# Centroids first, loads held, first routing ahead of the angles: the front of a fused attention and FFT-gate kernel

## The chip, the cores and the metric

The kernel runs on one core of one Trainium2 chip. The metric is device time in microseconds (us), as the median of repeated runs. A profiled execution gives a trace of every instruction with its start, its duration and what released it. The engines are TensorE (PE, its weight loads are PEld), VectorE (DVE), ScalarE (ACT), GpSimd (POOL) and SyncE (SP). Names that end in q (SPq, ACTq) are the instructions with which an engine issues transfers.

## The reference

Two operators follow one another. The first is attention in which each query sees only keys of its own cluster; B, H, S, D = 4, 8, 768, 64 and there are 16 centroids per head.

```python
q_assign = argmax(einsum('bhsd,hcd->bhsc', q_n, c_n))     # q_n, k_n, c_n: rows of length 1
k_assign = argmax(einsum('bhsd,hcd->bhsc', k_n, c_n))
mask = q_assign[:, :, :, None] == k_assign[:, :, None, :]
scores = where(mask, q @ k.T / sqrt(D), -1e9)
x = softmax(scores) @ v                                   # then heads side by side: [4, 768, 512]
```

The second takes x through a projection, a long convolution by FFT over the 768 positions, two gates and an output projection.

```python
x1, x2, x3 = split(x @ w_proj, 3)                          # 512 columns each
y = x1 * irfft(rfft(x2) * rfft(filter_fft)) * x3
out = y @ w_out
```

## The kernel before

The work is tiled by pairs of heads: 16 pairs, `p` from 0 to 15, each with six steps of 128 keys. A pair first goes through `routing(p)`, then six calls of `attend(p, sk)`, then `finish(p)`. After every fourth pair one batch is whole, and `hyena(b, ...)` does the convolution and gates of it. `inverse_tables` and `filter_tables` make the Fourier tables `inv` and `hm` once, near the start; both use the table `fw` that `angles` makes with sines on ScalarE.

`centroid()` loads the centroids (L427), divides each by its length in a chain of small VectorE operations with one square root on ScalarE, turns the result over on TensorE (L440) and copies it into `cbd` (L445).

`routing(p)` turns q and k over on TensorE (L600, twelve tiles, copied to `qkT` by ScalarE or VectorE), casts them to bfloat16 into `aug` on GpSimd (L309), multiplies with `cbd` (L617), copies the similarities to `sim`, turns them over (L625), and finds the nearest centroid of each row with five VectorE operations (L630 to L636), whose result is the one-hot tile `oh`. This is turned over again (L644), scaled into `ohT` (L649 or L651), and four transfers (L658) put its rows into `aug` beside the data. There they act as the cluster mask: the score product over `aug` (L320, called S here) carries a large negative term where the clusters differ.

`attend` is S into the PSUM tile `scores`, an exponential on ScalarE into `pb` (L681, three buffers), the product with v into `outs` (L691, called PV here), and an addition on VectorE that sums `pb` for the denominators (L701). The scores tile is single: the next S waits for the exponential of the last.

PSUM has eight banks. `scores` holds banks 0 to 2, `outs` 3 and 4, and three more are free for everything else. The pool `psF` gives such work a bank: 5, 6 and 7 at all times, and those of `scores` and `outs` as long as no S has been planned.

No loop order reaches the hardware as written. Each operation is recorded by `op(...)` with the engines that it may run on, a duration, a due time, and an earliest time `after`. `Plan.run` then takes operations one by one: on each engine the one with the smallest due time plus a charge (`WAIT`) for what it would make the engine wait, less a bonus (`SAME`) where TensorE stays in its mode. The order in which it takes them is the order of the engines' instruction queues, and on the chip each engine and each transfer queue works through its own in order. `behind` adds operations that must be taken earlier. `step(i)` is the planned time of attention step i, `ROUTE`, `LOAD`, `TABLES`, `FILTER`, `ANGLES` and `SPANS` shift the due times of the parts against it.

The loads of a pair are recorded by `load_pair`: q and k for two heads each (192 KB each) and v (384 KB), on SyncE's queue; of pair 0, k goes by ScalarE's queue, ahead of the centroids. The last lines of the kernel record the parts in this order: loads of pair 0, constants, centroid, loads of pair 1, angles, zeros, weights, and then the pairs, each with its routing.

Of the kernel before, what the change touches and what calls it, by code (L numbers as in the profile page):

```python
# [87 lines left out]
class BankPool:  # L88
# [45 lines left out]
class Plan:  # L134
# [36 lines left out]
    def run(self):  # L171
# [13 lines left out]
        while ready:  # L185
            best = {}
            for o in ready:
# [42 lines left out]
            if o.size:  # L230
                wire = max(wire, done) + o.size / 2.0e5
                done = wire
# [28 lines left out]
def kernel(  # L261
# [105 lines left out]
    psS, psO, psF, psD = (BankPool(banks, x) for x in ("S", "O", "F", "D"))  # L367
# [11 lines left out]
    def load(dst, src, size, due, w, e="SP", after=0.0):  # L379
        op(e, 0.65, lambda e: eng[e].dma_start(dst(), src), w=[w], due=due, size=size, kind="load", after=after)  # L380

    raws, vraws = {}, {}

    def load_pair(p):
        b, h = p // 4, 2 * (p % 4)
        for j, src in enumerate((q, k)):
            x = raws[p, j] = Val(raw)
            for hp in range(2):
                load(lambda x=x, hp=hp: x.t[:, :, hp], src[b, h + hp].rearrange("(p t) d -> p t d", t=NT),
                     196608, step(6 * p - LOAD) + j if p else -1000.0, (x, hp), "ACTQ" if p == 0 and j else "SP",  # L390
                     after=step(6 * p - LOAD) - 8.0 if p > 1 else 0.0)
        x = vraws[p] = Val(vraw)
        load(lambda x=x: x.t, v[b, h:h + 2].rearrange("h (p t) d -> p h (t d)", t=NT),
             393216, step(6 * p - 3), x, after=step(6 * p - 6) - 8.0 if p else 2.0)
# [27 lines left out]
    def centroid():  # L422
# [4 lines left out]
        op("ACTQ", 0.1, lambda e: nc.scalar.dma_start(c.t, centroids.rearrange("h c d -> (h c) d")), w=[c])  # L427
# [11 lines left out]
        cps = Val(psF)  # L439
# [91 lines left out]
    def filter_tables(due):  # L531
        lo, hi, ud = Val(k6), Val(k6), Val(k6)
        fv = moe_filter_fft.rearrange("(w p m e) d -> w e p m d", w=2, p=64, m=3, e=2)
        for e_ in range(2):
            for x, w in ((lo, 0), (hi, 1)):
                load(lambda x=x, e_=e_: x.t.rearrange("p (m d) -> p m d", m=3)[64 * e_:64 * e_ + 64], fv[w, e_], 393216, due - 8.0, (x, e_),
                     after=due - 20.0)
# [41 lines left out]
    def weights():  # L579
        op("POOL", 1.2, lambda e: nc.gpsimd.dma_start(wpj.t, moe_w_proj.rearrange("(t p) m -> p t m", p=128)),  # L580
           w=[wpj], due=step(20), size=3145728, lag=3.0, after=step(4))
        op("POOL", 0.8, lambda e: nc.gpsimd.dma_start(wout.t, moe_w_out.rearrange("(t p) m -> p t m", p=128)),
           w=[wout], due=step(24), size=1048576, lag=3.0, after=step(8))
# [4 lines left out]
    def routing(p):  # L588
        due = step(6 * p - ROUTE) if p else FIRST - 400.0
        g = p % 4  # L590
        aug = augs[p] = Val(augp)
        qkT = [Val(qkTp) for _ in range(2)]
        for j in range(2):
            for ch in range(2):
                ps = Val(psF)

                def f(e, j=j, ch=ch, ps=ps):
                    rv = raws[p, j].t.rearrange("p t h d -> p t (h d)")
                    for t in range(3):
                        nc.tensor.transpose(ps.t[:, ts(t, 128)], rv[:, 3 * ch + t], identp.t)  # L600
# [9 lines left out]
        ps = Val(psF)  # L610
# [10 lines left out]
        sT, mx, cand, m2, oh, ohT = Val(psF), Val(mxp), Val(candp), Val(m2p), Val(ohp), Val(ohTp)  # L621
# [16 lines left out]
        oT = Val(psF)  # L638
# [15 lines left out]
        for j in range(2):  # L654
            for hp in range(2):
                def f(e, j=j, hp=hp):
                    r0 = 32 * j + 16 * hp
                    eng[e].dma_start(aug.t[hp][j][64 - 16 * hp:80 - 16 * hp], ohT.t[r0:r0 + 16])  # L658
                op("ACTQ" if p == 0 and j else "SP", 0.6, f, r=[ohT], w=[(aug, ("m", hp, j))], due=due - 0.5 * (1 - hp),
                   kind="mask", size=24576)  # L660
# [214 lines left out]
    load_pair(0)  # L875
    constants()
    centroid()
    load_pair(1)
    angles()
    zeros()  # L880
    weights()
    for p in range(NP):
        if p + 2 < NP:
            load_pair(p + 2)
        routing(p)
        if p == 0:
            inverse_tables(step(TABLES))
            filter_tables(step(FILTER))
# [35 lines left out]
```

## Time and profile before

| what | value |
|---|---|
| median of three runs | 429.64 us (428.15 to 429.93) |
| the profiled execution: its own time | 428.38 us |
| its span in the trace | 426.6 us |
| TensorE busy (matmul) | 397.4 us, 93% of the span |
| VectorE busy | 349.1 us, 82% |
| ScalarE busy | 255.1 us, 60% |
| GpSimd busy | 116.8 us, 27% |
| transfers | 37.17 MB, 87 GB/s over the span |

The page of the profile gives busy time by engine and the busy share in 40 slices of 10.7 us. Matmuls are pipelined, so a busy TensorE is not one at its peak. The timeline lists instructions in order of time, those alike merged (x6), with the idle time of the engine before them and what ended it in square brackets. The windows give the busy time of each engine in stretches that one names, with the granted clock of TensorE (PEclk) and the mean busy share of the transfer engines. The chain of waits follows the work that ended last back to what released it.

### The profile page before, as it was taken

What the parts mean: (1) busy time and instruction counts of PE and PEld (TensorE: products, weight loads), DVE (VectorE), ACT (ScalarE), POOL (GpSimd) and SP (SyncE); (2) the same over time, 40 slices, a digit from 0 to 9 for tenths busy, and PEclk for the clock granted to TensorE, in tenths of its full rate; (3) what the DMA queues carried; (4) which work ended last, traced back from release to release, by engine and by line L of the source; (5) the groups of instructions that cost most, each with busy time, mean ns of one, the idle gap of its engine ahead of it and who ended that gap; (6) DMA issues with size and microseconds to landing.
All of it is one profiled execution on the core that took longest, in us unless ns stands there. A gap on an engine that the chain in (4) does not pass through costs nothing.

```text
span 426.6 us, 8705 instructions
## 1 busy us (share of the span) xinstructions
PE 397.4 (93%) x3485; PEld 212.7 (50%) x3485; DVE 349.1 (82%) x411; ACT 255.1 (60%) x318; POOL 116.8 (27%) x115
## 2 busy tenths in 40 slices
PE   2759999999999999999999999999999999799875
PEld 2425454454545556655445455545544555465542
DVE  2885997998989888989988798899998598557763
ACT  2387657677677757555665676666667744144342
POOL 5660403355156240512204160507211020001000
PEclk9898999999999999999999999999999999899999
DMA  9979804546254414111357311021201012100213
GB/s 185 187 177 210 193 21 112 132 105 158 50 141 87 99 42 120 42 37 39 91 178 185 76 31 43 11 77 49 75 3 40 5 38 98 40 12 2 98 51 148
DMA packets 68943, 37.17 MB, mean 87 GB/s; under 512 B 56940, under 2 KB 62632, under 8 KB 68904
## 3 DMA queue, kind: packets, MB, share of 16 engines
q1 hardware_dynamic: 66072, 34.06, 31.7%
q0 software_dynamic: 1056, 2.10, 2.7%
q10 hardware_dynamic: 1776, 0.48, 0.6%
q8 instruction: 27, 0.44, 0.5%
q14 instruction: 12, 0.10, 0.1%
HBM read 30.66 MB, written 6.48 MB: 87 GB/s over the span
## 4 chain that ended last, share of the span: by engine, by line
PE 86%; DVE 9%; ACT 2%; DMA 2%; issue 1%; ACTq 0%; DVEq 0%
PE outs L691 30%; PE scores L320 21%; PE bank L320 18%; PE bank L600 5%; PE bank L720 3%; PE bank L617 2%; PE outs L320 2%; DVE tm L796 2%; PE bank L625 2%; DMA c<-in_centroids_dram 1%; PE bank L528 1%; PE bank L644 1%; DVE yy L852 1%; DVE k L485 1%; DVE m L635 0%
## 5 line engine op out<-in xcount | busy, mean ns | idle before, releaser
L681 ACT ACTIVATE pb<-scores 128x1536 f32<-128x1536 f32 x96 | 139.3, 1451 | 48.3 <-PE scores L320 46.6
L691 PE MATMUL outs<-pb,vraw 128*64 128x512 f32 (+1 forms) x768 | 143.2, 493 | 0.2 <-ACT osb L711 0.2
L701 DVE TENSOR_TENSOR acc<-acc,pb 128x1536 f32<-128x1536 f32 x64 | 121.3, 1895 | 15.3 <-ACT pb L681 14.3
L309 POOL CAST aug<-qkT 64x768 bf16<-64x768 f32 x64 | 77.7, 1215 | 127.0 <-PE scores L320 76.1
L691 PEld LDWEIGHTS outs<-pb,vraw 128*64 128x64 f32 x768 | 53.5, 137 | 69.9 <-issue 63.8
L320 PE MATMUL scores<-aug,aug 128*64 128x512 bf16 (+3 forms) x768 | 81.5, 330 | 0.3 <-ACT pb L681 0.3
L320 PEld LDWEIGHTS <-aug 80*64 80x64 bf16 (+1 forms) x768 | 42.5, 110 | 30.1 <-issue 13.9
L309 POOL CAST xT<-rb 128x768 bf16<-128x768 f32 x10 | 18.8, 1882 | 80.9 <-DVE rb L756 56.1
L320 PEld LDWEIGHTS <-wpj 128*64 128x64 bf16 x512 | 31.3, 110 | 19.0 <-issue 7.1
L701 DVE TENSOR_TENSOR acc<-pb,pb 128x1536 f32<-128x1536 f32 x16 | 29.4, 1835 | 9.2 <-ACT pb L681 9.2
L320 PE MATMUL bank<-xT,wpj 128*64 128x384 bf16 x360 | 36.3, 327 | 0.0
L600 PE MATMUL bank<-ident,raw 128*128 128x128 f32 x171 | 27.9, 292 | 6.4 <-DMA raw<-in_q_dram 6.4
L320 PEld LDWEIGHTS <-k 128*64 128x64 bf16 (+1 forms) x448 | 22.0, 110 | 23.8 <-issue 11.9
L855 POOL TENSOR_TENSOR k<-yy,x 128x768 bf16<-128x768 f32 x6 | 11.1, 1857 | 63.1 <-DVE yy L852 60.7
L600 PEld LDWEIGHTS bank<-ident,raw 128*128 128x128 f32 x171 | 19.1, 145 | 18.3 <-issue 8.2
L307 ACT COPY qkT<-bank 128x384 f32<-128x384 f32 x47 | 21.2, 480 | 8.6 <-PE bank L600 6.7
L320 PE MATMUL bank<-wpj,uT 128*64 128x512 bf16 x168 | 21.4, 380 | 0.0
L796 DVE TENSOR_TENSOR tm<-bank,hm 128x1024 f32<-128x1024 f32 x16 | 19.2, 1217 | 0.9 <-issue 0.8
L711 ACT COPY osb<-outs 128x769 f32<-128x769 f32 x16 | 12.8, 798 | 11.7 <-PE outs L691 11.7
L761 DVE TENSOR_TENSOR uT<-rb 128x384 bf16<-128x384 f32 x32 | 19.5, 622 | 0.0
L756 DVE SCALAR_TENSOR_TENSOR rb<-osb,rb 128x768 f32<-128x768 f32 x16 | 16.0, 1003 | 0.8 <-DMA rb<-dr 0.8
L307 ACT CAST k<-bank 128x512 bf16<-128x512 f32 x20 | 11.7, 585 | 8.3 <-PE bank L320 8.0
(167 smaller groups left out, 448.9 us busy)
## 6 DMA issues: line engine op xcount, KB each, us to landing
raw<-in_q_dram SPq DMA_DIRECT2D x32, 192.0 KB, 4.5
vraw<-in_v_dram SPq DMA_DIRECT2D x16, 384.0 KB, 3.7
raw<-in_k_dram SPq DMA_DIRECT2D x30, 192.0 KB, 3.4
rb<-dr SPq DMA_DIRECT2D x30, 192.0 KB, 3.5
out_dram<-os SPq DMA_DIRECT2D x21, 256.0 KB, 2.1
k<-in_moe_filter_fft_dram SPq DMA_DIRECT2D x4, 384.0 KB
wpj<-in_moe_w_proj_dram POOLq DMA_DIRECT2D x1, 1536.0 KB, 13.8
aug<-ohT SPq DMA_DIRECT2D x62, 24.0 KB, 1.8
```

The source lines that it names most:

```text
L307: nc.scalar.copy(o, i)
L309: eng[e].tensor_copy(o, i)
L320: nc.tensor.matmul(out[64 * c:64 * c + 64], lhsT[:, 64 * c:64 * c + 64], rhs, **k)
L600: nc.tensor.transpose(ps.t[:, ts(t, 128)], rv[:, 3 * ch + t], identp.t)
L681: op("ACT", 1.48, lambda e: nc.scalar.activation(pb.t[:, :, :S], sps.t.rearrange("p (a b) -> p a b", a=2), Act.Exp, scale=0.125), r=[sps], ...
L691: nc.tensor.matmul(o.t[64 * hp:64 * hp + 64, lo:hi], vv.t[:, hp, ts(sk, D)], pb.t[:, hp, lo:hi], start=(sk == 0), stop=(sk == NT - 1))
L701: nc.vector.tensor_tensor(acc.t, a, pb.t[:, :, :S], op=Alu.add)
L711: op("ACT", 0.82, lambda e: nc.scalar.copy(osb.t, o.t[:, :S + 1]), r=[o], w=[osb], due=step(i) + 5.0)
L720: nc.tensor.matmul(dps.t[32 * z:32 * z + 32, :384], ones.t[:, :32], acc.t[:, hp, ts(ch, 384)], start=True, stop=True)
L756: op("DVE", 0.98, lambda e: V.scalar_tensor_tensor(rb.t, osb.t[:, :S], osb.t[:, S:S + 1], rb.t, op0=Alu.add, op1=Alu.mult), r=[osb, rb], w ...
L761: op("DVE", 0.55, lambda e, e_=e_, alu=alu: V.tensor_tensor(uT.t[:, e_], x3()[:, :, :64], x3()[:, :, 64:], op=alu), r=[rb], w=[(uT, e_)], ...
L796: op("DVE", 1.2, lambda e, i=i, cs=cs, ps=ps, tm=tms[cs]: V.tensor_tensor(tm.t, ps.t.unsqueeze(1).to_broadcast([128, 2, DM]), hm.t[:, i, c ...
```

## The change

Six things change, all in what is recorded for the planner.

- The centroids are recorded before the loads of pair 0 and are the first transfer on ScalarE's queue; k of pair 0 goes by SyncE's queue, behind q.
- `load` takes `behind`, and the loads of q, k and v, the filter's loads and the weights are recorded with `behind=masks0`, the four transfers of the first one-hot rows.
- `routing(0)` is recorded ahead of `angles()`.
- The first routing and the centroids take their banks from a new pool, `psE`, which may use those of `scores` and `outs` until the first S. The pool `psF` of all other work loses the banks of `scores` in that time, and keeps those of `outs`.
- Constants of the planner: `LOAD` from 18.19 to 24.14, `ANGLES` from 1.84 to 0.99, the start of the second span from 60.4 to 63.3, v of pair 0 due at 8.0 and not before 4.0.
- The planner's own durations: 0.4 for the issue of the centroids, 0.15 or 0.1 for a change of mode in place of 0.095, and transfers on ScalarE's queue no longer take the planner's wire.

```diff
-ROUTE, LOAD, TABLES, FILTER = 3.96, 18.19, 0.98, 1.79
-SPANS = ((42.9, 50.0), (60.4, 100.2), (88.8, 116.7), (95.5, 135.3))
+ROUTE, LOAD, TABLES, FILTER = 3.96, 24.14, 0.98, 1.79
+SPANS = ((42.9, 50.0), (63.3, 100.2), (88.8, 116.7), (95.5, 135.3))
-SAME, WAIT, ANGLES = 1.08, 82.17, 1.84
+SAME, WAIT, ANGLES = 1.08, 82.17, 0.99
...
-        quiet = not b.scores_begun or not b.scores_left
-        last = not b.outs_left
-        ok = [5, 6, 7] + ([0, 1, 2] if quiet else []) + ([3, 4] if not b.scores_begun or last else [])
+        ok = [5, 6, 7]
+        if not b.scores_begun:
+            ok += [3, 4] + ([0, 1, 2] if k == "E" else [])
+        if not b.scores_left:
+            ok += [0, 1, 2]
+        if not b.outs_left:
+            ok += [3, 4]
...
-                    start += 0.095
+                    start += 0.15 if o.mode == "A" else 0.1
...
-            if o.size:
+            if o.size and e != "ACTQ":
...
-    def load(dst, src, size, due, w, e="SP", after=0.0):
-        op(e, 0.65, lambda e: eng[e].dma_start(dst(), src), w=[w], due=due, size=size, kind="load", after=after)
+    def load(dst, src, size, due, w, e="SP", after=0.0, behind=()):
+        op(e, 0.65, lambda e: eng[e].dma_start(dst(), src), w=[w], due=due, size=size, kind="load", after=after,
+           behind=behind)
...
-                     196608, step(6 * p - LOAD) + j if p else -1000.0, (x, hp), "ACTQ" if p == 0 and j else "SP",
-                     after=step(6 * p - LOAD) - 8.0 if p > 1 else 0.0)
+                     196608, step(6 * p - LOAD) + j if p else -1000.0, (x, hp),
+                     after=step(6 * p - LOAD) - 8.0 if p > 1 else 0.0, behind=masks0)
...
-        op("ACTQ", 0.1, lambda e: nc.scalar.dma_start(c.t, centroids.rearrange("h c d -> (h c) d")), w=[c])
+        op("ACTQ", 0.4, lambda e: nc.scalar.dma_start(c.t, centroids.rearrange("h c d -> (h c) d")), w=[c])
...
+        psX = psF if p else psE
...
-                op("ACTQ" if p == 0 and j else "SP", 0.6, f, r=[ohT], w=[(aug, ("m", hp, j))], due=due - 0.5 * (1 - hp),
-                   kind="mask", size=24576)
+                x = op("ACTQ" if p == 0 and j else "SP", 0.6, f, r=[ohT], w=[(aug, ("m", hp, j))],
+                       due=due - 0.5 * (1 - hp), kind="mask", size=24576)
+                if p == 0:
+                    masks0.append(x)
...
-    load_pair(0)
     constants()
     centroid()
+    load_pair(0)
     load_pair(1)
+    routing(0)
     angles()
```

`masks0` is a list that `routing(0)` fills, and `behind` is read when an operation is recorded. The loads of pairs 0 and 1 are recorded ahead of `routing(0)` and so are not held; those of pairs 2 and later, the filter's and the weights are. In the built program q and k of pairs 0 and 1 and v of pair 0 stand on SyncE's queue ahead of its two mask transfers, and v of pair 1 and all other loads behind them.

More of the change, by code (lines that the diff above doesn't have):

```diff
@@ L366 @@
                   [psum.tile([128, 512], F32, name=f"bank{i}") for i in range(3)])
-    psS, psO, psF, psD = (BankPool(banks, x) for x in ("S", "O", "F", "D"))
+    psS, psO, psF, psD, psE = (BankPool(banks, x) for x in ("S", "O", "F", "D", "E"))
     banks.scores_left, banks.outs_left = NP * NT, NP
@@ L536, in filter_tables @@
                 load(lambda x=x, e_=e_: x.t.rearrange("p (m d) -> p m d", m=3)[64 * e_:64 * e_ + 64], fv[w, e_], 393216, due - 8.0, (x, e_),
-                     after=due - 20.0)
+                     after=due - 20.0, behind=masks0)
         fu = lambda: ud.t.bitcast(BF16)[:, :1536]
@@ L580, in weights @@
         op("POOL", 1.2, lambda e: nc.gpsimd.dma_start(wpj.t, moe_w_proj.rearrange("(t p) m -> p t m", p=128)),
-           w=[wpj], due=step(20), size=3145728, lag=3.0, after=step(4))
+           w=[wpj], due=step(20), size=3145728, lag=3.0, after=step(4), behind=masks0)
         op("POOL", 0.8, lambda e: nc.gpsimd.dma_start(wout.t, moe_w_out.rearrange("(t p) m -> p t m", p=128)),
-           w=[wout], due=step(24), size=1048576, lag=3.0, after=step(8))
+           w=[wout], due=step(24), size=1048576, lag=3.0, after=step(8), behind=masks0)
     augs = {}
@@ L620, in routing @@
         op(("ACT", "DVE"), (0.486, 0.55), lambda e: copy(e, sim.t, ps.t[:, :384]), r=[ps], w=[sim], due=due)
-        sT, mx, cand, m2, oh, ohT = Val(psF), Val(mxp), Val(candp), Val(m2p), Val(ohp), Val(ohTp)
+        sT, mx, cand, m2, oh, ohT = Val(psX), Val(mxp), Val(candp), Val(m2p), Val(ohp), Val(ohTp)
         def f(e):
@@ L637, in routing @@
            r=[cand, m2], w=[oh], due=due, shared=True)
-        oT = Val(psF)
+        oT = Val(psX)
         def f(e):
@@ L884 @@
             load_pair(p + 2)
-        routing(p)
-        if p == 0:
+        if p:
+            routing(p)
+        else:
             inverse_tables(step(TABLES))
```

10 lines of the change are left out of this document (5 added, 5 removed).

## The prediction

> **What bounds the kernel now.** I read the windows first, to find where TensorE is not full, then the chain of waits in the front, then the timeline of it.
>
> ```profile
> 0.00:10.00 10.00, 2.79 (x12) 2.42 (x12) 2.21 (x12) 2.61 (x5) 5.53 (x24) 1.00 0.98 174
> 10.00:20.00 10.00, 6.78 (x41) 3.94 (x42) 7.97 (x18) 2.68 (x6) 6.01 (x8) 0.83 1.16 223
> 20.00:30.00 10.00, 6.76 (x46) 3.52 (x43) 9.18 (x16) 7.78 (x14) 6.62 (x15) 1.00 0.63 147
> 30.00:40.00 10.00, 8.07 (x71) 5.33 (x68) 5.05 (x9) 8.00 (x9) 2.14 (x3) 0.83 1.02 212
> 40.00:50.00 10.00, 10.00 (x85) 4.72 (x84) 9.81 (x8) 6.07 (x8) 3.04 (x2) 1.00 0.98 200
> ```
>
> The first number after the width is TensorE's busy time. It lacks 15.6 us up to 40 and nothing after that; the waits of TensorE from 34 to 380 us, the largest of which follows, are a few tenths in the attention and the rest near 360.
>
> ```profile
> PE scores L320 <- DVE tm L796: 2.2, 2, 1.4
> ```
>
> So from about 33 us on the kernel is bound by TensorE, and a change to the front is worth what it takes off the time at which TensorE becomes full, less the work that is then still undone. The chain of waits and the timeline show what the front waits for.
>
> ```profile
> 0.75 2.75 SPq L380 DMA_DIRECT2D raw<-in_q_dram  x4
> ...
> 2.42 5.40 DMA c<-in_centroids_dram
> ...
> 6.36 2.16 PE L600 MATMUL bank<-ident,raw 128*128 128x128 f32 x9 [6.36 <-DMA raw<-in_q_dram]
> ...
> 11.05 0.33 DVE L438 TENSOR_SCALAR cn<-c,s 128x64 f32<-128x64 f32 x1
> ...
> 12.25 0.44 DVE L445 COPY cbd<-scores 64x64 f32<-64x64 f32 x2
> ...
> 12.83 1.50 PE L617 MATMUL scores<-qkT,cbd 128*32 128x384 f32 x8 [1.09 <-DVE cbd L445]
> 14.27 1.54 PE L600 MATMUL outs<-ident,raw 128*128 128x128 f32 x6
> ...
> 16.44 0.56 DVE L630 TENSOR_REDUCE mx<-bank 128x24 f32<-128x384 f32 x1 [1.57 <-PE bank L625]
> ...
> 18.61 0.56 DVE L636 TENSOR_TENSOR oh<-cand,m 128x384 bf16<-128x384 bf16 x1
> ...
> 20.26 0.99 ACT L649 ACTIVATE ohT<-scores,mk 64x768 bf16<-64x768 bf16 x1 [1.22 <-PE scores L625]
> ...
> 21.97 0.83 ACTq L658 DMA_DIRECT2D aug<-ohT  x1
> ...
> 26.93 0.88 PE L600 MATMUL scores<-ident,raw 128*128 128x128 f32 x6 [2.30 <-DVE cand L631]
> ...
> 29.43 0.84 PE L320 MATMUL scores<-aug,aug 80*64 80x512 bf16 x8
> ...
> 30.54 1.28 ACT L681 ACT_TABLE_LOAD   x1
> ...
> 31.84 1.45 ACT L681 ACTIVATE pb<-scores 128x1536 f32<-128x1536 f32 x1
> ...
> 34.99 1.45 ACT L681 ACTIVATE pb<-scores 128x1536 f32<-128x1536 f32 x1 [0.95 <-PE scores L320]
> 37.29 0.38 PE L320 MATMUL scores<-aug,aug 80*64 80x512 bf16 x1
> ```
>
> The centroids land at 7.82, and the first routing goes through the similarities at 12.83 to the one-hot tile, whose last mask transfer is issued at 21.97. S0, the first score product, could run soon after, but stands on TensorE's queue behind transposes of pair 3 (26.93) that wait for the `scores` banks, on VectorE work that itself stood behind the angles. It starts at 29.43; S2, the third, at 37.29.
>
> **The change part by part.** I follow the built program's queues with the durations above.
>
> *The centroids.* They are issued at 0.75 instead of 2.42, with nothing ahead of them on their queue. The present 5.40 us to landing is the upper bound; the lower is that of a mask transfer of nearly this size:
>
> ```profile
> DMA to landing us min/median/max: 2.2/2.2/2.2
> ```
>
> So they land between 2.95 and 6.15. I take 3.3, near the lower, since the load of q alone shares the wires. From landing to the end of `cn` VectorE's order is unchanged: 11.38 − 7.84 = 3.54, so `cn` ends at 6.85. The two copies into `cbd` now precede the 0.56 us copy of `qkT`, which they follow today: 12.69 − 11.38 − 0.56 = 0.75, to 7.6.
>
> *k of pair 0 goes behind q on SyncE's queue.* Two issues more there, some 0.7 us each: four loads took 2.75 us to issue. q then has the wires nearly alone, and with 0.4 MB at the 174 GB/s of the first window it lands no later than today's 6.36; k lands about 2 us behind the front of q. Its six transposes follow the centroids' one on TensorE: 6 × 2.16/9 = 1.44 from 7.15, to 8.6, and the last copy to 9.2. This is the new cover: centroids later than 3.3 cost the same amount, k later than 7.1 too.
>
> *First routing.* From the similarities (12.83) to the first maximum (16.44) stand the same operations, among them six transposes of pair 1: 3.61, from 9.25 to 12.85. VectorE has five angle operations ahead of that maximum, about 3.3 us from 9.2, so they fit, barely. Maximum to the end of `ohT` is 16.44 to 21.25, 4.81, so 17.65. The masks go out at once; the second on ScalarE's queue started 0.69 behind the first and lands 2.2 later: S0 at 20.6. Of the 8.8 us that it gains, 3.6 come from the routing and 5.2 from TensorE's order, for no work of pairs 2 and 3 stands before it now: their loads are issued only behind the masks on SyncE's queue.
>
> *ScalarE between the first two exponentials.* This is the wait that comes. The angles, still 5 to 6 us of VectorE behind the one-hot tile, end near 21.5, and the sines now stand between the first exponential and the second, with a table load on either side: four table loads in all, three today.
>
> ```profile
> L491 ACT ACTIVATE fw<-k,quarter 128x384 bf16<-128x384 f32 x3 | 1.8, 603 | 0.0
> L494 ACT ACTIVATE fw<-k 128x384 bf16<-128x384 f32 x3 | 1.5, 508 | 0.0
> L491 ACT ACT_TABLE_LOAD x1 | 1.3, 1283 | 0.0
> L681 ACT ACT_TABLE_LOAD x1 | 1.3, 1283 | 0.0
> ```
>
> The first exponential runs from 21.5 to 22.95; then 1.28 + 3 × 0.603 + 3 × 0.508 + 1.28 + 1.45 = 7.34, so the second ends at 30.3 and S2 starts there. Its lead over 37.29 is 6.9 to 7.0. Behind ScalarE wait S2 and the inverse tables; TensorE has in that gap S1, one one-hot transpose, twelve transposes of pair 2, one PV, a similarity and four groups of the inverse tables, some 6.6 us, if q and k of pair 2 have landed: issued from 19 us on, 1.2 MB with v of pair 1 at 200 GB/s is 6 us, to 27. That leaves it full from 25 on, nearly free of waits.
>
> *The work postponed.* Ahead of S2 today, and behind it in the changed program: pair 2's turned similarities (0.55), its one-hot transposes (0.52), two groups of inverse tables (2 × 0.53) and six transposes of pair 3 (0.88):
>
> ```profile
> 28.50 0.52 PE L644 MATMUL outs<-identb,oh 128*64 128x128 bf16 x6 [0.69 <-DVE oh L636]
> 28.95 0.55 PE L625 MATMUL outs<-ident,sim 128*128 128x128 f32 x3
> 33.15 0.53 PE L516 MATMUL bank<-identb,fw 128*64 128x128 bf16 x6 [0.40 <-DVE inv L309]
> ```
>
> Together 3.0 us, which TensorE does later, when it is full: 7.0 − 3.0 = 4.0 net.
>
> *The order of the rest.* The whole program is re-planned. Where only a PV stands between two score products, TensorE waits for the exponential:
>
> ```profile
> 56.47 0.84 PE L320 MATMUL scores<-aug,aug 80*64 80x512 bf16 x8 [0.25 <-ACT pb L681]
> ```
>
> There are two such short steps more, 0.5 us; changes of TensorE's mode are 187 for 184, under 0.3. I set 0.6, with ±1.5 for an end whose operations are the same and whose order differs. The new start of the second span and `LOAD` show only in this order.
>
> The sum: 7.0 − 3.0 − 0.6 = 3.4. The profiled execution took 428.38, so 425.0; the median shown is 1.26 above it, which would make 426.2. I forecast 425.6, between the two.
>
> **A cold TensorE.** At 14 to 16 and at 34 to 36 the granted clock is half:
>
> ```profile
> 14.00:16.00 2.00, 2.00 (x12) 1.73 (x9) 0.87 (x2) 0.63 (x2) 0.19 (x1) 0.50 1.13 228
> 34.00:36.00 2.00, 2.00 (x12) 1.12 (x10) 0.08 (x1) 1.05 (x2) 0.00 (x0) 0.50 1.07 201
> ...
> 34.70 2.42 PE L691 MATMUL outs<-pb,vraw 128*64 128x512 f32 x8
> ...
> 37.94 1.59 PE L691 MATMUL outs<-pb,vraw 128*64 128x512 f32 x8
> ```
>
> Those eight matmuls took 2.42 against 1.59, and with S1 ahead of them the stretch cost some 1.5 us, inside today's 37.29. In the changed front a slow stretch may fall behind S2 instead, and the gain is then 1.9. The Trainium skill, "TensorE: Matmul & The Clock Gate", Part 1, says that the clock is halved until about 3.4 us of sustained work, and again after a pause; by that rule the pause before S0 chills S0 and S1, which ScalarE's 7.34 us hide, and the sum stays. The trace agrees only in part: it grants full speed from 0 to 10 us.
>
> **The rivals.**
>
> *The filter's loads come late.* They move from 11.6 and 28.9 us to behind the loads of pairs 2 and 3, some 25 to 28, and meet the weights, which GpSimd issues near 30 as today.
>
> ```profile
> 28.94 1.20 SPq L380 DMA_DIRECT2D k<-in_moe_filter_fft_dram  x2
> ...
> 30.46 0.92 POOL L580 DMA_DIRECT2D wpj<-in_moe_w_proj_dram  x1
> ...
> 41.86 1.75 DVE L540 TENSOR_TENSOR k<-k,k 128x1536 bf16<-128x1536 f32 x1
> ...
> vraw<-in_v_dram SPq DMA_DIRECT2D x1, 384.0 KB, 14.3
> ```
>
> VectorE meets the filter's sum (L540) at about 38, ahead of the additions that free `pb`, with 1.3 us to spare until TensorE needs its result. Today's second pair landed without making it wait, 13 us after issue at most. By the 14.3 us of the v load beside them the last would land at 42.5: 3.3 us of stall, the gain gone, 428.3. By the 200 GB/s they land near 37. From 39.3 on each microsecond is lost.
>
> *The early S0 is empty.* On the other side: if the masks do not land early, S2 still stands 9.7 us behind S0, for the sines and two table loads now stand between. The gain of 7.0 less the 3.6 of later costs is gone when S0 is at 24.0. With centroids at their upper bound (2.85 later) it is 23.5; add VectorE, whose five angle operations then run under GpSimd's casts at 0.9 to 1.0 each, and 1.5 more is at hand: 25.0, or 429.4. With S0 at 26, which also takes masks stuck behind the loads, 430.4. For it speaks how tightly VectorE is packed; against it, that the mask transfers find no load in flight.
>
> *A switch of tables costs twice its load.* Each of the two between the exponentials at 2.56 instead of 1.28 puts S2 at 32.9, and the sum at 427.6. Against it: the exponential at 31.84 follows its 30.54 table load without a pause. The Trainium skill, "ScalarE: Activation LUTs", "What ACT_TABLE_LOAD costs", adds a drain of 1.38 us to the load of 1.283 and so speaks against the change, by 2.8 us here. The trace agrees with the load and shows no drain.
>
> **How the numbers follow.** A median of this kernel tells about 0.5% (2.1 us) from no change. The case above has 0.64, most of it faster, 422.5 to 427.5. Filter late: 0.13, about no change. Tables twice: 0.05, no change or just faster. Empty S0, or an order of the rest that loses more than 3 us: 0.18, 429 to 432. Faster 0.64, same 0.18, slower 0.18. For 8 in 10 the range must reach into the rivals: from 421.5, the lead undiminished by clock and order, to 430.5.
>
> **What would show it.** Right: centroids landing by 3.5, S0 near 20.6 with no transposes of pairs 2 and 3 ahead, exponentials 7.3 apart at 21.5 and 28.8, S2 near 30.3, TensorE full from there on and the filter's sum on VectorE without a wait. Wrong: S0 after 24, VectorE waiting for a transfer at the filter's sum, a slow clock beyond 30, or more than 4 us of TensorE's waits between 40 and 380.

## The result and the profile after

The changed kernel takes 423.38 us (median of four runs, 422.92 to 424.17) against 429.77 (428.15 to 429.93) before on the same chip: 0.9862 of the time, with a 95% interval from 0.9834 to 0.989. This ratio, like those below, is estimated from all runs and is not the quotient of the two medians. The forecast was 425.6, faster, within 421.5 to 430.5. The profiled execution took 422.92, with a span of 421.1. Lines of code behind the changed functions are shifted: S is now L324, the exponential L689, PV L699, the filter's sum L545, the spectrum multiplications L804.

The windows of the changed kernel, with the same columns as before:

```profile
0.00:10.00 10.00, 4.57 (x20) 2.99 (x21) 4.99 (x22) 2.92 (x5) 5.54 (x24) 1.00 0.85 177
10.00:20.00 10.00, 5.04 (x38) 2.55 (x33) 9.83 (x16) 4.32 (x8) 8.81 (x16) 0.91 0.09 28
20.00:30.00 10.00, 8.05 (x44) 4.82 (x45) 5.16 (x11) 8.70 (x11) 1.79 (x4) 0.57 1.04 214
30.00:40.00 10.00, 9.64 (x93) 5.00 (x91) 9.42 (x14) 6.43 (x9) 3.27 (x4) 1.00 1.05 216
```

TensorE lacks 12.7 us up to 40 where it lacked 15.6. The sixth group, the granted clock, is 0.57 from 20 to 30: this front runs its first score products at about half speed. In the second window the transfers have a share of 0.09, since the loads are held. The timeline shows the first routing:

```profile
2.57 0.23 DVE L433 TENSOR_TENSOR c<-c 128x64 f32<-128x64 f32 x1 [0.99 <-DMA c<-in_centroids_dram]
...
8.60 2.72 PE L623 MATMUL scores<-qkT,cbd 128*32 128x384 f32 x8
...
13.43 0.54 DVE L636 TENSOR_REDUCE mx<-scores 128x24 f32<-128x384 f32 x1
...
17.06 0.99 ACT L655 ACTIVATE ohT<-scores,mk 64x768 bf16<-64x768 bf16 x1 [1.65 <-PE scores L650]
...
20.34 1.49 PE L324 MATMUL scores<-aug,aug 80*64 80x512 bf16 x8 [2.85 <-DMA aug<-ohT]
...
21.87 1.45 ACT L689 ACTIVATE pb<-scores 128x1536 f32<-128x1536 f32 x1 [1.24 <-PE scores L324]
...
25.52 1.54 PE L606 MATMUL bank<-ident,raw 128*128 128x128 f32 x6
26.99 2.26 PE L699 MATMUL outs<-pb,vraw 128*64 128x512 f32 x8
27.52 1.28 ACT L689 ACT_TABLE_LOAD   x1
28.81 1.45 ACT L689 ACTIVATE pb<-scores 128x1536 f32<-128x1536 f32 x1
...
32.14 0.84 PE L324 MATMUL scores<-aug,aug 80*64 80x512 bf16 x8
...
39.88 1.75 DVE L545 TENSOR_TENSOR k<-k,k 128x1536 bf16<-128x1536 f32 x1
```

S0 is at 20.34, and the wait that ends last before it is that for the masks; the two exponentials are 6.94 apart; S2 is at 32.14 where it was at 37.29; the filter's sum has no wait in front of it. S2 follows tables, similarities and transposes on TensorE without a pause, 1.88 us behind the end of the second exponential (30.26). The waits of TensorE from 33 to 345 us (total, count, longest) are small:

```profile
PE bank L650 <- DVE oh L642: 1.3, 1, 1.3
PE scores L324 <- ACT pb L689: 0.7, 2, 0.4
PE outs L699 <- ACT osb L719: 0.2, 1, 0.2
```

The surprise is at the other end of the kernel. Here is the timeline of before (rows of TensorE and VectorE) from the last denominators, L741, to the first projection of the last batch, which makes `outs` from `wpj` and `uT`; after it the timeline of the changed kernel with the same stations:

```profile
349.50 1.46 PE L741 MATMUL scores<-acc,ones 128*64 128x384 f32 x8
...
363.93 0.84 PE L528 MATMUL scores<-k,fw 128*64 128x512 bf16 x6
365.34 0.84 PE L528 MATMUL scores<-k,fw 128*64 128x512 bf16 x6 [0.57 <-ACT x L822]
367.55 1.85 PE L320 MATMUL scores<-wout,k 128*64 128x512 bf16 x8 [1.37 <-DVE tm L796]
369.13 1.98 PE L320 MATMUL outs<-wout,k 128*64 128x512 bf16 x8
...
369.44 1.23 DVE L796 TENSOR_TENSOR tm<-scores,hm 128x1024 f32<-128x1024 f32 x1 [1.94 <-PE scores L320]
...
373.25 0.84 PE L320 MATMUL outs<-wpj,uT 128*64 128x512 bf16 x6
```

```profile
348.45 1.48 PE L749 MATMUL scores<-acc,ones 128*64 128x384 f32 x8
...
360.34 0.84 PE L533 MATMUL outs<-k,fw 128*64 128x512 bf16 x6
360.99 0.84 PE L533 MATMUL scores<-k,fw 128*64 128x512 bf16 x6
...
362.42 1.21 DVE L804 TENSOR_TENSOR tm<-scores,hm 128x1024 f32<-128x1024 f32 x1
...
366.97 0.84 PE L324 MATMUL outs<-wpj,uT 128*64 128x512 bf16 x6
```

Of S2's 5.15 us only 1.05 are left at the last denominators (their place varies by about 1 us between executions of one order: with the changed order up to there it is 349.43 in e4_end_old, below). From there to the first projection of the last batch it is 23.75 before and 18.52 after, 5.23 less; from that projection to the last product 48.2 and 49.11, 0.91 more. In these two executions most of the gain therefore comes from a stretch that no line of the diff names.

### The profile page after: what moved, and what is told of

It reads as the page before. It is cut to its first block, busy times and chain, and to the rows that moved or that the text cites. A ratio compares the mean times of both kernels' runs of the same rounds, so it can differ in the third digit from the quotient of the medians.

```text
span 421.1 us, 8711 instructions
## 1 busy us (share of the span) xinstructions
PE 393.9 (94%) x3485; PEld 213.6 (51%) x3485; DVE 354.4 (84%) x414; ACT 256.5 (61%) x317; POOL 120.9 (29%) x114
## 5 line engine op out<-in xcount | busy, mean ns | idle before, releaser
L689 ACT ACTIVATE pb<-scores 128x1536 f32<-128x1536 f32 x96 | 139.4, 1452 | 52.2 <-PE scores L324 50.9
L699 PE MATMUL outs<-pb,vraw 128*64 128x512 f32 (+1 forms) x768 | 143.2, 492 | 0.2 <-ACT osb L719 0.2
L313 POOL CAST aug<-qkT 64x768 bf16<-64x768 f32 x64 | 85.1, 1329 | 160.6 <-PE scores L324 80.3
L709 DVE TENSOR_TENSOR acc<-acc,pb 128x1536 f32<-128x1536 f32 x64 | 118.1, 1845 | 9.5 <-ACT pb L689 9.1
L699 PEld LDWEIGHTS outs<-pb,vraw 128*64 128x64 f32 x768 | 54.4, 137 | 66.2 <-issue 59.7
L324 PE MATMUL scores<-aug,aug 128*64 128x512 bf16 (+3 forms) x768 | 81.8, 332 | 5.1 <-DMA aug<-ohT 2.8
L324 PEld LDWEIGHTS <-aug 80*64 80x64 bf16 (+1 forms) x768 | 42.1, 111 | 35.0 <-issue 15.5
L324 PEld LDWEIGHTS <-wpj 128*64 128x64 bf16 x512 | 32.3, 110 | 16.6 <-issue 5.6
L324 PE MATMUL bank<-xT,wpj 128*64 128x384 bf16 x384 | 38.5, 326 | 0.0
L709 DVE TENSOR_TENSOR acc<-pb,pb 128x1536 f32<-128x1536 f32 x16 | 31.8, 1987 | 4.7 <-ACT pb L689 4.7
L606 PE MATMUL bank<-ident,raw 128*128 128x128 f32 x183 | 30.5, 294 | 5.5 <-DMA raw<-in_q_dram 5.4
L324 PEld LDWEIGHTS <-k 128*64 128x64 bf16 (+1 forms) x448 | 21.7, 108 | 22.3 <-issue 11.4
L863 POOL TENSOR_TENSOR k<-yy,x 128x768 bf16<-128x768 f32 x7 | 16.1, 2302 | 58.6 <-DVE yy L860 54.1
L606 PEld LDWEIGHTS bank<-ident,raw 128*128 128x128 f32 x183 | 20.6, 147 | 20.1 <-issue 11.5
L313 POOL CAST xT<-rb 128x768 bf16<-128x768 f32 x8 | 10.6, 1325 | 45.3 <-PE bank L324 20.1
L769 DVE TENSOR_TENSOR uT<-rb 128x384 bf16<-128x384 f32 x32 | 21.4, 680 | 0.1
L324 PE MATMUL bank<-wpj,uT 128*64 128x512 bf16 x160 | 20.6, 380 | 0.0
L804 DVE TENSOR_TENSOR tm<-bank,hm 128x1024 f32<-128x1024 f32 x16 | 19.4, 1219 | 0.8 <-PE bank L533 0.7
L764 DVE SCALAR_TENSOR_TENSOR rb<-osb,rb 128x768 f32<-128x768 f32 x16 | 17.8, 1114 | 0.0
L324 PEld LDWEIGHTS <-uT 128*64 128x64 bf16 x192 | 12.6, 109 | 8.6 <-issue 1.9
```

Of the source, the lines that this page charges most:

```text
L313: eng[e].tensor_copy(o, i)
L324: nc.tensor.matmul(out[64 * c:64 * c + 64], lhsT[:, 64 * c:64 * c + 64], rhs, **k)
L689: op("ACT", 1.48, lambda e: nc.scalar.activation(pb.t[:, :, :S], sps.t.rearrange("p (a b) -> p a b", a=2), Act.Exp, scale=0.125), r=[sps], ...
L699: nc.tensor.matmul(o.t[64 * hp:64 * hp + 64, lo:hi], vv.t[:, hp, ts(sk, D)], pb.t[:, hp, lo:hi], start=(sk == 0), stop=(sk == NT - 1))
L709: nc.vector.tensor_tensor(acc.t, a, pb.t[:, :, :S], op=Alu.add)
L764: op("DVE", 0.98, lambda e: V.scalar_tensor_tensor(rb.t, osb.t[:, :S], osb.t[:, S:S + 1], rb.t, op0=Alu.add, op1=Alu.mult), r=[osb, rb], w ...
```

## The experiments

The planner's choices were written out as two tables, old and new, of the same 1563 operations (operation, engine, buffers), and the loop of `Plan.run` was replaced by one that takes operations in the order of a table. Experiments are tables put together from the two, or one of them with a few rows moved. All but e5_warm, which adds products that nothing reads, do the same work. Their code lies lower in the file: L372 (L371) is L324 of the changed kernel, L581 is L533, L593 is L545, L662 (L653) is L606, L795 is L749, L850 (L849) is L804. "Before" is each time the median of before on the same chip. The experiments ran on several chips, so differences of under 1 us between runs of different groups are read with care.

**Which part of the program the gain comes from.** Four tables, cut either at the first S of pair 4 (some 100 us) or at the last denominators:

```diff
 e1_front_new:  -old            +new to pair 4's first S, old behind it
 e2_front_old:  -new            +old to pair 4's first S, new behind it
 e3_end_new:    -old            +old to the last denominators, new behind them
 e4_end_old:    -new            +new to the last denominators, old behind them
```

> The order of the changed program up to the start of pair 4's first score product, the order of the old one from there on. If the front carries the whole gain, as the prediction has it: about 424, 5 to 6 us under before. If the front carries only what its trace shows (S2 5.15 us earlier, 3.0 us of work postponed): about 427.5, 2 us under before, and the rest comes from the order of the end.

> The mirror: the old order up to pair 4, the changed program's order from there on. If the front carries the whole gain: no change, 429. If the end carries some 4 us: about 425.5, 4 us under before.

> The old order up to the last pair's denominator product, the changed program's order for what is left (some 75 us). By the two traces this stretch up to the last batch's first projection took 22.3 us before and 17.2 after, with one group of gate products (0.65) fewer: if that is a matter of its order, 4 us under before, 425.5; if it follows from what the middle left over, no change, 429.

> The changed program up to the last denominator product, the old order for what is left. If the order of the end carries 4 us: 427.5, 4 us above the changed kernel; if the front carries all: 423.5, as the changed kernel.

| table | front, to pair 4 | middle | end | us | ratio, 95% |
|---|---|---|---|---|---|
| before | old | old | old | 429.5 | 1 |
| e1_front_new | new | old | old | 427.6 | 0.9968 (0.9944 to 0.9993) |
| e4_end_old | new | new | old | 427.87 | 0.9961 (0.9944 to 0.9978) |
| e2_front_old | old | new | new | 426.0 | 0.9924 (0.9907 to 0.9941) |
| e3_end_new | old | old | new | 425.37 | 0.9911 (0.9889 to 0.9933) |
| after | new | new | new | 423.38 | 0.9862 (0.9834 to 0.989) |

The last row is the result above, whose own before was 429.77; the others ran together. Each of the four lies within 0.5 us of the time that its expectation gives for an end worth some 4 us.

The new end is worth 429.5 − 425.37 = 4.1 with all else old and 427.87 − 423.38 = 4.5 with all else new. All ahead of it is worth 1.6 (429.5 − 427.87) or 2.0 (425.37 − 423.38), and the middle nothing that shows (427.6 to 427.87, 425.37 to 426.0). The stretch from the last denominators to the first projection keeps to the end's order, whatever stands ahead of it; first e3_end_new, then e4_end_old:

```profile
351.90 1.48 PE L795 MATMUL scores<-acc,ones 128*64 128x384 f32 x8
...
370.42 0.84 PE L372 MATMUL outs<-wpj,uT 128*64 128x512 bf16 x6
```

```profile
349.43 1.48 PE L795 MATMUL scores<-acc,ones 128*64 128x384 f32 x8
...
372.95 0.84 PE L372 MATMUL outs<-wpj,uT 128*64 128x512 bf16 x6
```

18.52 and 23.52 (the expectation of e3_end_new counts from the end of the denominators, hence its smaller numbers). The front is thus shown to be the smaller part of the gain.

**What in the end it is: the banks.** The three banks of `scores` are one tile. In the rows of before, ScalarE's copy, the spectrum products, the multiplications and the output product all use `scores`, and each waits for the one planned ahead of it: the second spectrum product (bank 2) for the copy (bank 0, 0.57), the output product (bank 0) for the first multiplication (bank 1, 1.37), the second multiplication (bank 2) for the output product (bank 0, 1.94). None of the three waits for its own bank.

```diff
 e9_one_bank, in the old table
-second spectrum product of the last block  bank 2 (scores)
-second output product behind it            bank 3 (outs)
+second spectrum product of the last block  bank 3 (outs)
+second output product behind it            bank 2 (scores)
```

> The kernel before, with two bank numbers exchanged near its end: the last of the six spectrum products of the third batch goes to bank 3, in the tile outs, instead of bank 2, in scores, and the second output product behind it to bank 2 instead of bank 3. Every engine's order of instructions is the old one. Theory (the three banks of scores are one tile, and every access to it, on whichever engine, waits for the one planned before it): TensorE no longer waits for ScalarE's copy between the two spectrum products (0.57) and waits less ahead of the output products (1.37); VectorE's second multiplication starts near 366 instead of 369.44, the stretch of half clock at 369 to 371 goes, and the time from the last denominators to the first projection of the last batch falls from 23.75 to 20 to 21.5: 426 to 427.5 in all, 2.3 to 3.7 less than before on the same chip. Rival (the order of the work there, how many projections stand behind the spectrum products, decides): the time stays within 0.7 of before, and the 23.75 stays above 23.

```profile
364.66 0.84 PE L581 MATMUL scores<-k,fw 128*64 128x512 bf16 x6
365.31 0.84 PE L581 MATMUL outs<-k,fw 128*64 128x512 bf16 x6
367.33 1.92 PE L372 MATMUL scores<-wout,k 128*64 128x512 bf16 x16 [1.18 <-DVE tm L850]
```

428.29, 0.9978 (0.9962 to 0.9994): 1.2 less than 429.47. The wait of 0.57 and the half clock are gone (both output products take 1.92 together, where they took 1.85 and 1.98), the second multiplication follows the first at 367.19, 2.25 sooner although the denominators are 0.7 later, and the stretch falls from 23.75 to 22.47. Part of what is won goes to two other waits of `scores` products for ScalarE's copies of the outputs, 0.67 and 0.72 behind 369, where before has one of 0.27. That is between what the two sides expected: the shared tile costs, but one bank is not the whole of it.

**What in the end it is: the order.**

```diff
 e12_end_order, in the table of e4_end_old
 last denominators
+both spectrum products of the middle block
 output products, projections ...
-both spectrum products of the middle block
 ...
-projection A
 both spectrum products of the last block
+projection A
+projection B
 two output products
-projection B
```

> New order up to the last denominators and the old order behind them, with three things moved within that old end as the new one has them: the two spectrum products of the second frequency block of the third batch right behind the last denominators (their two multiplications and the addition on VectorE likewise earlier), and two projections of the third batch from ahead of the last block's spectrum products, and from behind the output products, to between the two. Bank numbers stay the old ones except for the four products that this needs. Theory (the end gained by the order: the convolution's multiplications start earlier, and two projections fill TensorE's wait for the last of them): from the last denominators to the first projection of the last batch 18.5 to 20.5 instead of 23.52, and 423.5 to 425.5 in all against the 427.87 of the same order without the moves. Rival (the bank numbers and the half clock that follow from them): 22.3 to 23.5, and 426.8 to 428.

425.93, 0.9929 (0.9916 to 0.9943), 1.9 less than e4_end_old; against the before of its own chip (428.75) it gains 2.8 where e4_end_old gained 1.6, so 1.2 is the safer figure. From its timeline, rows of TensorE and VectorE:

```profile
365.61 1.49 PE L581 MATMUL scores<-k,fw 128*64 128x512 bf16 x12
...
369.57 0.84 PE L372 MATMUL scores<-xT,wpj 128*64 128x384 bf16 x8 [1.83 <-DVE tm L850]
...
371.31 1.22 DVE L850 TENSOR_TENSOR tm<-scores,hm 128x1024 f32<-128x1024 f32 x1 [1.79 <-PE scores L372]
...
374.66 0.84 PE L372 MATMUL outs<-wpj,uT 128*64 128x512 bf16 x6
```

The last denominators are at 353.45 in this execution, so the stretch is 21.21: 2.3 of the 5.0 between 23.52 and 18.52 come with these moves, less than the theory wanted and more than the rival. The run moves the middle block's products and the two projections together and does not tell which counts. The last block's products now stand 12.2 us behind the denominators (14.4 in the old order, 11.9 in the new). With the old bank numbers the second multiplication still starts 5.7 us behind those products, 2.1 in the changed kernel. The other 2.7 lie in the bank numbers and the few rows not moved; how they divide was not run.

**A better version.** If the shared tile costs time in the last 40 us as well, new bank numbers alone should help the changed kernel.

```diff
 e11_banks, in the new table, 15 rows; among them, in the last batch
-spectrum products, middle block: 2, 0 (scores, scores)
-spectrum products, last block:   7, 2
-last output products:            0, 3 (scores, outs)
+spectrum products, middle block: 7, 5 (tiles of their own)
+spectrum products, last block:   7, 5
+last output products:            6, 7
```

> The changed kernel, with other bank numbers for 17 products of the last batch, chosen so that products whose readers are slow lie in tiles of their own (banks 5, 6, 7) and not beside others in scores or outs; every engine's order stays. Theory (false waits between the banks of one tile cost time in the end): TensorE's waits for tm at 385.6 (1.66) and 392.1 (1.31) shrink to under 0.7 each, the last multiplications end 2 to 4 us sooner, and the time is 419.5 to 422. Rival (VectorE's own work bounds that stretch, or the waits are real): 422.7 to 424.

The expectation speaks of 17 products; 15 rows of the table differ, 13 products of the last batch and two output products of the third.

419.43 (418.18 to 420.03), 0.9771 (0.974 to 0.9802): 4.0 less than the changed kernel, 3.7 when each is taken against its own before, with no instruction in another place. The multiplications of the last batch on VectorE, first the changed kernel, then this one:

```profile
390.84 1.22 DVE L804 TENSOR_TENSOR tm<-scores,hm 128x1024 f32<-128x1024 f32 x1 [1.55 <-PE scores L324]
393.00 1.23 DVE L804 TENSOR_TENSOR tm<-scores,hm 128x1024 f32<-128x1024 f32 x1 [0.93 <-PE scores L324]
...
400.12 1.23 DVE L807 TENSOR_TENSOR k<-tm,tm 128x1024 bf16<-128x1024 f32 x1
```

```profile
388.89 2.35 DVE L849 TENSOR_TENSOR tm<-bank,hm 128x1024 f32<-128x1024 f32 x2 [0.53 <-PE bank L371]
...
396.15 1.23 DVE L852 TENSOR_TENSOR k<-tm,tm 128x1024 bf16<-128x1024 f32 x1
```

Two waits for `scores` become one of 0.53, and the last addition is 4.0 earlier although the last denominators are 0.4 later (348.89). TensorE's waits for `tm` behind 380, 3.0 in the changed kernel, are 0.9.

**The front, part by part.** First the clock. Two windows of the changed kernel:

```profile
18.00:20.00 2.00, 0.00 (x0) 0.00 (x0) 1.97 (x5) 0.70 (x2) 1.37 (x2) 0.57 0.13 27
...
26.00:28.00 2.00, 2.00 (x9) 1.05 (x10) 1.33 (x3) 1.98 (x5) 0.28 (x1) 0.50 1.29 218
```

All windows of 2 us from 20 to 28 show 0.50. e5_warm adds products to keep TensorE busy around S0:

```diff
 one-hot transposes of pair 0
+16 products of 384 columns into a free bank
 S0
+8 products of 384 columns
 S1
```

> The changed kernel, order untouched, with 16 products of 384 columns that nothing reads on TensorE ahead of the first score product S0, and 8 more ahead of the second. They stand where TensorE is idle (17.5 to 20.3 and 21.8 to 23.4). If the half clock from 18 to 28.5 us is what puts S2 at 32.1 instead of 30.3, it is granted in full there now, S2 stands near 30.5 and the kernel gains up to 1.6 us over the changed one (422). If the pause is not what lowers the clock, or S2 is held by ScalarE's sines and table loads: no change or up to 0.5 us slower.

```profile
26.25 0.87 PE L662 MATMUL bank<-ident,raw 128*128 128x128 f32 x6 [2.12 <-DMA raw<-in_q_dram]
```

```profile
20.00:24.00 4.00, 3.54 (x31) 2.04 (x30) 3.22 (x7) 3.12 (x3) 0.00 (x0) 1.00 0.73 185
24.00:28.00 4.00, 1.88 (x15) 1.01 (x14) 1.69 (x3) 3.97 (x8) 0.01 (x1) 1.00 0.91 199
```

The clock stays at 1.00, S0 stays at 20.34, and S2 comes at 31.45, 0.7 sooner; 422.74, 0.9854 (0.9829 to 0.988), which can't be told from the changed kernel. At full clock TensorE has 2.1 us to spare from 24 to 28, waiting for q of pair 2 until 26.25, and behind that it has 5.2 us of transposes, PV, similarities and tables ahead of S2. In the changed kernel, at half clock, q is in use at 25.52 after a wait of 0.31. So the 0.7 is not the price of the half clock: with the clock up, the load of q takes its place as what holds S2. e8_unheld, below, is the other half of this.

Then the place of the first two score products. e6_sines_first puts the sines ahead of the first exponential (one table load less) and S1 and the first PV behind the transposes and tables:

```diff
-exp0, sines, exp1 on ScalarE; S0, S1, transposes, PV0, tables, S2 on TensorE
+sines, exp0, exp1 on ScalarE; S0, transposes, tables, S1, PV0, S2 on TensorE
```

> The changed kernel with the six sines on ScalarE ahead of the first exponential, so that one table load falls away, and with the second score product and the first PV behind the transposes of pair 2 and four groups of inverse tables on TensorE. If the wait of 7.3 us between the first two exponentials is the price of the new order: the second exponential ends about 1.3 us earlier (29.0), S2 follows, and the kernel gains about 1 us (422.5). If S2 is set by TensorE's slow clock and its own work before S2: no change. If the first score product was worth its early place: slower by 1 to 2 us.

425.99, 0.9914 (0.9885 to 0.9943), 2.6 more than the changed kernel, though the two intervals just touch: S1 moves to 31.30, the second exponential waits 5.50 us for it, and S2 moves to 33.68. The run moves the sines and, on TensorE, S1 and the first PV together, so it shows that the two early score products as a whole earn their place, and not what the sines alone cost.

Then the queues. In e7_k_first the two loads of k of pair 0 go back to ScalarE's queue. In the built program they stand there behind the centroids, not ahead of them, so it tests only which queue k takes, not the centroids' place; e10_k_ahead puts them ahead.

```diff
 e7_k_first:  ScalarE's queue  centroids +k +k     SyncE's queue  q q -k -k
 e10_k_ahead: ScalarE's queue  +k +k centroids     SyncE's queue  q q -k -k
```

> The changed kernel with k of pair 0 back on ScalarE's queue ahead of the centroids, all else as it is. The centroids then land some 5 us later (7.8 instead of 2.6) and the first routing and S0 follow by 3 to 4 us; as S2 stands 11.8 us behind S0, it comes at 35 to 36 and the whole gain of the front (1.5 to 2 us) is gone: 426 to 427. If S2 has slack, under 1 us lost.

> The changed kernel, with both loads of k of pair 0 on ScalarE's queue ahead of the centroids, as before the change; all else keeps its order. Theory (the transfers of one queue are done in order, so the centroids come 2 to 4 us later, and with them the whole first routing): centroids first used at 5 to 7 instead of 2.57, S0 at 22.5 to 24.5, S2 1.5 to 4 later than 32.14 and the time 425 to 427.5. Rival (the first routing is paced by k and by VectorE, and the centroids have slack): S0 within 1 us of 20.34 and the time within 1 us of the changed kernel's 423.4.

e7_k_first: 424.8, 0.9895 (0.9873 to 0.9918), 1.4 more than the changed kernel, at the edge of what the two intervals tell apart. The centroids are used at 2.64. With k on the other queue, and q of pair 1 next behind q of pair 0, q is there at 6.49 instead of 5.40; S0 follows at 21.48 and S2 at 33.65. e10_k_ahead: 428.32, 0.998 (0.9959 to 1.0), all but before's time:

```profile
7.23 0.23 DVE L481 TENSOR_TENSOR c<-c 128x64 f32<-128x64 f32 x1 [5.64 <-DMA c<-in_centroids_dram]
...
24.18 1.61 PE L372 MATMUL scores<-aug,aug 80*64 80x512 bf16 x8 [2.83 <-DMA aug<-ohT]
...
44.83 1.76 DVE L593 TENSOR_TENSOR k<-k,k 128x1536 bf16<-128x1536 f32 x1 [1.85 <-DMA k<-in_moe_filter_fft_dram]
```

The centroids come 4.66 later, S0 3.84, S2 (at 35.16) 3.0, the time 4.9. Part of that is the filter's load, which VectorE now meets 1.85 us before it has landed.

Last, the held loads:

```diff
 e8_unheld, SyncE's queue
+v of pair 1, q and k of pairs 2 and 3
 two mask transfers of pair 0
-v of pair 1, q and k of pairs 2 and 3
```

> The changed kernel with v of pair 1 and q and k of pairs 2 and 3 issued on SyncE's queue ahead of the first mask transfers instead of behind them. If holding them is what gets the masks through: masks and S0 1 to 3 us later. If the wires would be clear by 17 us in any case (2 MB from 8 us on at 200 GB/s ends at 18 to 19): S0 as it is, the transposes of pair 2 no longer wait for loads, 0 to 1 us gained.

424.46, 0.9902 (0.9872 to 0.9932). S0 is at 20.51 and S2 at 32.14 as in the changed kernel, though the transfers' share from 10 to 20 us is 1.14 instead of 0.09. Here the masks land as fast beside the loads; holding them buys S0 nothing. The transposes of pair 2 wait for no load now, but they start at 25.66 all the same, because the clock is 0.50 from 20 to 28 here too and the work ahead of them takes that long. The 1.1 by which the median is above the changed kernel's is not told from none: the two intervals overlap.

The two runs together say more than each alone. With the clock up and the loads as they are (e5_warm), q of pair 2 holds S2; with the loads early and the clock at half (e8_unheld), TensorE's slow work holds it. No run has both out of the way. An estimate from the rows of e5_warm: the one-hot transposes end at 24.13, 5.2 us of work behind them would end at 29.3, and the second exponential ends at 29.87, so S2 would start near 29.9 and wait for ScalarE, as I had forecast.

## Why the prediction was right, and where it was not

The sign, the range and, within 2.2 us, the time were right. The sum was not: the lead of the front was less than I had put, the end gained where I had put a loss, and the two went against each other. That the time came so near is luck to that extent: with the end's old order the same front takes 427.87, which is inside the range too, but only 1.6 under before.

- *The centroids and the first routing.* First use 2.57 for a landing at 3.3, `cn` at 6.15 for 6.85, similarities 8.60 for 9.25, `ohT` to 18.05 for 17.65, S0 20.34 for 20.6. The routing gave back more than the 0.65 of the similarities: its first maximum came at 13.43 for 12.85, behind similarities that took 2.72 where they had taken 1.50; the masks then landed faster than forecast. e10_k_ahead shows that this front needs the centroids first: with k ahead of them its gain is gone, and more.
- *ScalarE between the exponentials.* 21.87 and 28.81 for 21.5 and 28.8, since the six sines overlap and take 2.86 us for the 3.33 of the sum. The table load at 27.52 ends at 28.80 and the exponential starts at 28.81: the rival of tables that cost twice did not come. The drain that the Trainium skill, "ScalarE: Activation LUTs", "What ACT_TABLE_LOAD costs", adds is not in this trace.
- *S2 at 30.3, lead 7.0.* This step failed: 32.14, and 5.15. I let ScalarE's second exponential release S2, which ended at 30.26 as forecast. But TensorE still had work ahead of S2: the transposes of pair 2, PV0, similarities and tables. I had listed that work as some 6.6 us, at full clock, that left TensorE full from 25 on; what came was q of pair 2 in use at 25.52 and half clock until 28.5. e5_warm and e8_unheld show that either of the two is enough to keep S2 late (31.45 and 32.14). The landing was loosely worked as well: 6 us from 19 on end at 25 and not at 27.
- *A cold TensorE.* By the rule of the Trainium skill, "TensorE: Matmul & The Clock Gate", Part 1, I had S0 and S1 chilled and ScalarE hiding it. The trace agrees on S0 and S1 (0.50 from 20 to 28). But the work behind S1 was chilled too: S1, the one-hot transposes, the first six transposes of pair 2 and PV0 took 1.49, 0.84, 1.54 and 2.26, and 0.84, 0.50, 0.87 and 1.51 in e5_warm, 2.4 us less. That is more than ScalarE could hide. I also held against the rule that the trace grants full speed from 0 to 10 us; that was a misreading, as the last section shows.
- *The work postponed, 3.0, and the attention's order.* From S2 to the last denominators 4.1 of the 5.15 are lost, give or take the 1 us by which that place varies. The 3.0, which no run measures by itself, and the growth of TensorE's waits from S2 to 345, 2.2 where they were 0.5, make 4.7. The largest single one, 1.3, is a one-hot transpose behind VectorE. By the exchanged tables the front and middle are worth 1.6 to 2.0, not 3.4.
- *The order of the rest, "0.6, with ±1.5 for an end whose operations are the same and whose order differs".* This is the term that was mis-sized most: the end gave 4.1 to 4.5. I had the waits near 360 in view, in the row of 2.2 us in all, and took them for TensorE's whole loss. What stood there was a chain over three engines through one tile; it also delayed VectorE's second multiplication of the last block by 1.94, and half clock followed it (e9_one_bank, without the 0.57 and with 1.18 for 1.37, kept full clock). Equal operations did not mean equal time.
- *The filter's loads.* No wait in the profiled execution of the changed kernel. But the rival is real: in the profiled execution of e12_end_order, whose front is the same, VectorE waits as long as it said (3.3).

```profile
42.81 1.76 DVE L593 TENSOR_TENSOR k<-k,k 128x1536 bf16<-128x1536 f32 x1 [3.16 <-DMA k<-in_moe_filter_fft_dram]
```

  That execution took 429.8, the other five of that kernel 425.48 to 426.71; the profiled one of e1_front_new, with 3.31 at the same place, 431.42, the other eleven 425.7 to 428.62. None of the changed kernel's four runs was like that.
- *The empty early S0.* Its break-even point was S0 at 24.0. e10_k_ahead has S0 at 24.18 and 428.32, with the end's gain of 4 in it: without that it would be slower than before (428.32 + 4.1 against 429.47, also with the 1.85 of the filter's wait taken off), which is argued from the exchanged tables and was not run. The mechanism is there; the centroids kept it away.

What stays open: where S2 would be with full clock and early loads together; whether the 2.7 that e12_end_order leaves lie in bank numbers or in rows not moved; and what decides from one execution to the next whether the filter's load is late.

## What to carry to other kernels

Where a planner re-plans the whole program, a change at one end must be priced at the other too: exchange the orders at a cut, both ways, before the gain is put down to the lines that were edited. Where several banks are one tile, each access waits for the one planned ahead of it on any engine; look for waits on a tile whose own bank is long free, and give products with slow readers tiles of their own (3.7 to 4.0 us here for 15 rows of bank numbers). When a wait is removed, list what the next engine's queue still holds ahead of the instruction, with the landing time of its operands and the clock that it will run at, before taking the release as the start. When a run removes one of two such limits and little happens, the other may have taken its place.

## What was not expected of the hardware

- A granted clock of 1.00 in a window need not mean full speed. The windows of the changed kernel show 1.00 from 0 to 10, but the products in it took the time of half speed: six transposes 1.51 us at 5.40 and again at 7.16, as at 25.52 (1.54, clock 0.50) and against 0.88 at 29.18 (clock 1.00).

```profile
7.16 1.51 PE L606 MATMUL outs<-ident,raw 128*128 128x128 f32 x6
...
29.18 0.88 PE L606 MATMUL bank<-ident,raw 128*128 128x128 f32 x6
```

  The clock records that the trace holds begin at about 11.5 us; for the time before them the window shows 1.00 without a record.
- In the changed kernel the clock fell to half near 18.3, 0.8 us into the pause of 2.85 us ahead of S0, and came back near 28.5, although TensorE was busy for 3.93 of the 4 us from 24 to 28. In the end of before a pause of 1.37 us was followed by half speed:

```profile
369.00:371.00 2.00, 2.00 (x10) 0.89 (x7) 1.56 (x2) 0.26 (x1) 0.00 (x0) 0.50 0.00 0
```

  With 1.18 in the same place, e9_one_bank kept 1.00; but so did e12_end_order, from 367 to 371, with a pause of 1.83 there. The length of one pause does not decide it.
- A transfer of 32 KB that is first on its queue was in use 1.8 us after its issue at 0.75, with q's loads beside it. Behind two loads of 192 KB on the same queue (e10_k_ahead) it was in use 4.8 us after its issue at 2.43.
